# Merged row-half groups and two-block runs of the heads' products in a gated mix of linear attention and a SwiGLU FFN

## The chip, the cores and the metric

One core of a Trainium2 (trn2) chip runs one program. The metric is its time on the device in microseconds, the median of several executions. Five engines work beside each other, each through its own queue in order: TensorE (PE, with its weight loads PEld), VectorE (DVE), ScalarE (ACT), GpSimd (POOL), and SyncE (SP), which here only issues DMAs. They wait for one another by semaphores. PE writes to PSUM, eight banks of 128 partitions by 512 f32 values; POOL can't read it, so ACT and DVE empty it.

## The reference

For 2048 tokens of 640 features (bf16), two branches are mixed by a gate:

```
q, k, v = split(x @ wqkv)                      # 32 heads of 20
phi(q)  = [softmax(q w_phi), softmax(-q w_phi)]   # 40 features per head; the same for k
kv = sum over tokens of phi(k)^T v ;  z = sum over tokens of phi(k)
o  = (phi(q) kv) / (phi(q) z + 1e-6)
a  = o @ wo
b  = (silu(x @ w_gate) * (x @ w_up)) @ w_down     # 1728 hidden values
g  = sigmoid(sum(x * gate_w))
out = g * a + (1 - g) * b
```

## The kernel before

**Order by hand.** The kernel is written out step by step. `ORDER` is a list of letters with indices; each letter calls one function, which records its instructions on the engines, and a tracker adds the semaphore waits that the addresses call for. So the list sets the order in each engine's queue, and nothing reorders it later. All matmuls are recorded by `mm` (L300), all ACT operations by `actop` (L318), DVE and POOL operations by `copy` (L324), `tt` (L328), `stt` (L332) and `reduce` (L339), all DMAs by `dma` (L353, L354).

**Tiles and blocks.** Tokens go in 16 tiles of 128; four tiles make a block, counted from 0 to 3. The first part (until the letter Z) loads, makes the values (V) and the keys' features (K, S, P), and sums kv and z (E). The part from Z on, which the change touches, has these steps:

- Q t: the queries' products of tile t on PE (ten matmuls of 320 columns) and two exponentials on ACT into eq. A, B, C: sums and products on DVE (`qsum`, `qden`, `qscale`; C is six DVE instructions, ending in qc). c: the scaling on POOL into ph, and a transposing DMA on SP into phiT, which has room for two blocks.
- F b.k: chunk k (128 of the 1728 hidden values) of the FFN for block b: ten matmuls of 512 columns into a pair of banks, tanh and a copy on ACT, a product on DVE and one on POOL, into hT (128 x 512). hT has two buffers of 14 chunks, for blocks of even and odd number. Chunk 13 has only 64 hidden values; its tokens are laid in both row halves of the chunk (two tiles in rows 0 to 63, two in rows 64 to 127).
- O b.p and o b: the heads' products phi(q) kv of block b, part p of three. Each head pair fills only 64 columns of the array, so two matmuls run side by side on the column halves. The result goes to oT by ACT. The odd last group (40 columns) goes to ol, and o issues four small DMAs on SP that move it into oT.
- W b.p: chunk 13's down projection for two tiles of a block. Its contraction is 64 rows long, so two matmuls, one for each tile, run side by side on the row halves. W opens the accumulation of the two tiles: it takes a pair of PSUM banks for each, which D keeps adding to.
- D b.u: down projection of tile u of block b: 13 chunks against wd and 5 groups of oT against wog, each in two parts of 320 columns, then ACT's scaling by the gate into osb and the store on SP. Tile 15 ends the kernel; its second part is cut into 224 and 96 columns, to shorten the last eviction.

PSUM's eight banks are used as four pairs; a step takes the pair used longest ago (`next_pair`). In before, W stands eight times (two per block), and the O's of a block stand together, so there are four runs of them. A stage of F's is followed by a stage of D's of a block, block after block.

Of the kernel before, what the change touches and what calls it, by code (L numbers as in the profile page):

```python
# [1 line left out]

# [1 line left out]

# [4 lines left out]
P = 128  # L9
S_TOK = 2048  # L10
D = 640
# [4 lines left out]
NB = 4  # L16
# [25 lines left out]
U0.3 U1.3 U2.3 U0.4 U1.4 U2.4 V3 Y F0.1 M1 i3 M0 F0.0 M2 V4 M3 M4 K0 K1 I S0 V6 V5 S1 P0 K3 K2 P1 E0  # L42
V9 K4 E1 S3 V7 P3 K5 S2 V8 V10 S4 P2 P4 E2 R0 E3 K6 S5 P5 S6 i4 E4 V14 K7 K8 P6 V15 S7 R2 E5 K9 S8
P7 R1 E6 K10 S9 V12 P8 E7 P9 K11 S10 P10 F0.2 R3 F1.2 E8 E9 K12 E10 S11 S12 K14 S14 V11 K13 P11 P12
E11 K15 P14 R4 S13 P13 F1.9 S15 P15 E12 V13 T F1.8 E13 F1.11 E14 Q1 E15 Q0 Q2 N Z A1 A0 J A2 F0.7
F0.9 F1.4 B0 F1.12 B1 F0.4 L C0 F1.7 c0 F1.10 C1 F0.5 B2 c1 F0.11 Q3 C2 F1.0 F0.8 c2 F0.10 B3 Q4
F1.6 A3 C3 Q5 c3 F1.3 F0.13 F0.12 A4 F0.3 B4 F1.5 F0.6 O0.2 O0.1 O0.0 o0 C4 F1.1 F1.13 B5 A5 C5 Q6
c4 Q7 c5 Q8 W0.0 B7 A6 B6 C6 A7 c6 D0.1 D0.0 Q9 C7 W0.1 B8 A8 D0.2 C8 c7 Q10 D0.3 F2.10 F2.9 F2.2 c8
O1.2 A9 O1.1 B9 O1.0 B10 F2.8 o1 C9 Q11 c9 F2.5 F2.11 F2.4 Q12 B11 F2.3 A10 C10 B12 F2.7 A11 C11
W1.1 D1.3 D1.2 A12 c11 c10 Q14 W1.0 D1.0 A14 C12 D1.1 Q13 F3.2 F3.3 c12 O2.2 O2.1 B13 B14 O2.0 o2  # L50
F2.13 A13 F3.12 F3.5 F2.1 C14 Q15 F3.4 F3.9 F2.12 C13 F2.0 A15 c13 F2.6 c14 B15 F3.1 F3.0 F3.6 C15
c15 F3.13 W2.0 F3.7 D2.1 D2.0 F3.11 O3.2 O3.0 O3.1 F3.8 o3 F3.10 W2.1 D2.3 W3.0 D3.0 D3.1 D2.2 W3.1
D3.2 D3.3
"""


# [143 lines left out]
def _build(nc, A_x, A_wqkv, A_w_phi, A_wo, B_x, B_w_gate, B_w_up, B_w_down, gate_w, out):  # L200
# [5 lines left out]
    def sb(name, shape, dtype):  # L206
        t = nc.alloc_sbuf_tensor(name, list(shape), dtype)
        tr.reg(t, "sbuf", nc.lookup_mloc(t).addr)
        return t
# [9 lines left out]
    ident = sb("ident", [P, P], BF16)  # L219
    us = sb("us", [P, 3, 512], BF16)  # L220
    osb = sb("osb", [P, 4, D], BF16)
    ol = sb("ol", [P, 256], BF16)
    kvsb = sb("kvsb", [P, NCH, 64], BF16)
    hmask = sb("hmask", [P, 3], F32)
    zt = sb("zt", [P, NCH, 3], F32)
# [16 lines left out]
    qd = sb("qd", [P, 2, 32], F32)  # L242
    qc = sb("qc", [P, 2, 66], F32)
    hT = sb("hT", [P, 2, 14, 512], BF16)

    wdbase = nc.lookup_mloc(wd).addr
    v1x = nc.alloc_sbuf_tensor_at("v1x", [P, NT - NV, 33 * 21], BF16, offset=wdbase)
    tr.reg(v1x, "sbuf", wdbase)

    def vbuf(t):  # L250
        return v1r[:, t, :] if t < NV else v1x[:, t - NV, :]
# [28 lines left out]
    def bank(b, c0, c1, r0=0, r1=P):  # L280
        return ps[r0:r1, b * 512 + c0:b * 512 + c1]
# [62 lines left out]
    def memset(e, a, v):  # L344
        eo = tr.eng[e]
        return run(e, lambda: eo.memset(a, v), [], [a])
# [67 lines left out]
    def fills(i):  # L414
        if i < 2:
            v1v = (v1r, v1x)[i][:, :, :].rearrange("p b (h d) -> p b h d", d=DH + 1)
            memset("pool", v1v[:, :, H, :], 0.0)
            memset("pool", v1v[:, :, :, DH:DH + 1], 1.0)
        elif i == 2:
            memset("pool", ekr[:, :, 1280:FK], 0.0)  # L420
            memset("pool", krec[:, :, :], 0.0)
        elif i == 3:
            memset("pool", kvsb[:, :, :], 0.0)
            memset("pool", eq[:, :, 1280:FP], 0.0)
            memset("pool", qc[:, :, :], 0.0)
            memset("pool", hmask[:, :], 1.0)
            select(hmask[:, :], [[-40, 3]], ALU.is_ge, 0.0, 0, 1)
            select(hmask[:, :], [[40, 3]], ALU.is_gt, 0.0, 40, -1)
        else:
            memset("pool", ph[:, :, :], 0.0)  # L430
            memset("pool", zh[:, NCH:P], 0.0)
# [225 lines left out]
           ALU.mult)  # L657
        dma("sp", phiT[:, (t // 4) % 2, t % 4, :, :], ph[:, b, :], transpose=True)

    def oitem(bt, part):  # L660
        buf = bt % 2
        pr = next_pair()
        pairs = []
        ms = [2 * part, 2 * part + 1]
        for i, m in enumerate(ms):
            for s in range(2):
                j = 2 * m + s
                if j >= NCH:
                    continue
                if j == NCH - 1:  # L670
                    for g, p0 in enumerate((0, 64)):
                        pairs.append((bank(2 * pr + i, 256 * g, 256 * g + 256, p0, p0 + 40),
                                      kvsb[0:80, j, 0:40], phiT[0:80, buf, 2 * g:2 * g + 2, j, :],
                                      True, True, False))
                    continue
                else:
                    l, o = kvsb[0:120, j, :], bank(2 * pr + i, 0, 512, 64 * s, 64 * s + 64)
                    r = phiT[0:120, buf, :, j, :]
                pairs.append((o, l, r, True, True, False))
        mm(pairs)  # L680
        if part < 2:
            copy("act", oT[:, buf, 2 * part:2 * part + 2, :], halves(pr, 512))
        else:
            copy("act", oT[:, buf, 4, :], bank(2 * pr, 0, 512))
            copy("act", ol[0:40, :], bank(2 * pr + 1, 0, 256, 0, 40))
            copy("act", ol[64:104, :], bank(2 * pr + 1, 256, 512, 64, 104))

    def omove(bt):
        for g in range(2):
            for s in range(2):  # L690
                dma("sp", oT[64 * s + 60:64 * s + 64, bt % 2, :, 256 * g:256 * g + 256],
                    ol[64 * g + 20 * s:64 * g + 20 * s + 20, :])


    nus = [0]

    def fitem(bt, k):
        buf = bt % 2
        pr = next_pair()
        xr = [xT[:, 4 * bt:4 * bt + 4, c, :] for c in range(5)]  # L700
        u = us[:, nus[0] % 3, :]
        nus[0] += 1
        if k < 13:
            g, up = bank(2 * pr, 0, 512), bank(2 * pr + 1, 0, 512)
            h = hT[:, buf, k, :]
            mm(group(g, [(wg[:, c, P * k:P * k + P], xr[c]) for c in range(5)]))
            mm(group(up, [(wu[:, c, P * k:P * k + P], xr[c]) for c in range(5)]))
        else:
            pairs = []
            for b in range(2):  # L710
                pairs += group(bank(2 * pr + b, 0, 256),
                               [(wt[:, c, P * b:P * b + P], xT[:, 4 * bt + b:4 * bt + 4:2, c, :]) for c in range(5)])
            mm(pairs)
            for b in range(2):
                r0, r1 = 64 * b, 64 - 64 * b
                h, g = hT[r0:r0 + 64, buf, k, 0:256], bank(2 * pr + b, 0, 256, r0, r0 + 64)
                actop(h, g, ACTF.Tanh, 0.5)
                actop(u[r0:r0 + 64, 0:256], bank(2 * pr + b, 0, 256, r1, r1 + 64), ACTF.Copy)
                stt(h, h, 1.0, g, ALU.add, ALU.mult)
            h = hT[:, buf, k, 0:256]  # L720
            tt("pool", h, h, u[:, 0:256], ALU.mult)
            return
        if bt == 2:
            for _ in range(NWAIT):
                act.wait_ge(tr.sem["pe"], 1)
        actop(h, g, ACTF.Tanh, 0.5)
        actop(u, up, ACTF.Copy)
        stt(h, h, 1.0, g, ALU.add, ALU.mult)
        tt("pool", h, h, u, ALU.mult)
# [8 lines left out]

    def parts(t):

        pr = dpr[t]
        if t < NT - 1:
            return [(2 * pr[0], 0, 320), (2 * pr[0] + 1, 320, D)]
        return [(2 * pr[0], 0, 320), (2 * pr[0] + 1, 320, 544), (2 * pr[1], 544, D)]

    def hitem(bt, p):

        todo = []
        for b in range(2):
            t = 4 * bt + 2 * p + b  # L750
            dpr[t] = [next_pair() for _ in range(1 + (t == NT - 1))]
            held.update(dpr[t])
            r = slice(64 * b, 64 * b + 64)
            todo.append([(bank(k, 0, c1 - c0), hT[r, bt % 2, 13, P * p:P * p + P], wd[r, 13, c0:c1], True, False, False)
                         for k, c0, c1 in parts(t)])
        mm([m for ab in zip_longest(*todo) for m in ab if m])

    def ditem(bt, u):
        buf = bt % 2
        t = 4 * bt + u  # L760
        tok = slice(P * u, P * u + P)
        ls = [(hT[:, buf, k, tok], wd[:, k, :]) for k in range(13)]
        ls += [(oT[:, buf, m, tok], wog[:, m, :]) for m in range(5)]
        n = len(ls)
        cols = [[(bank(k, 0, c1 - c0), l, r[:, c0:c1], False, i == n - 1, False) for i, (l, r) in enumerate(ls)]
                for k, c0, c1 in parts(t)]
        held.difference_update(used(r) for r in dpr[t])
        o = osb[:, t % 4, :]
        if t < NT - 1:
            mm([p for ab in zip(*cols) for p in ab])  # L770
            actop(o.rearrange("p (b c) -> p b c", b=2), halves(dpr[t][0]), ACTF.Copy, omg[:, t:t + 1])
            stores_done()
            out_evs.append(dma("sp", out2[t * P:(t + 1) * P, :], o))
            return
        for (b, c0, c1), e, ms in zip(parts(t), ("sp", "sp", "act"), cols):
            mm(ms)
            if e == "act":
                run("dve", lambda: dve.tensor_scalar(o[:, c0:c1], bank(b, 0, c1 - c0), omg[:, t:t + 1], None,  # L778
# [11 lines left out]
    def kv_end():  # L790
# [9 lines left out]
        "f": lambda i: load_ffn(FCUT[i], FCUT[i + 1]), "L": load_late_weights, "T": tail_weights, "J": gates,  # L800
        "Y": w_blocks, "I": kv_begin, "N": kv_end, "Z": z_row,
        "Q": qtile, "A": qsum, "B": qden, "C": qscale, "c": qmul,
        "F": fitem, "O": oitem, "o": omove, "W": hitem, "D": ditem,
    }
    for w in LOADS.split() + ORDER.split():
        ops[w[0]](*[int(a) for a in w[1:].split(".") if a])
# [45 lines left out]
```

## Time and profile before

| what | us |
|---|---|
| median of 3 runs | 287.82 |
| lowest and highest | 287.75 and 288.12 |
| the profiled execution | 289.13 |
| its span, from the first instruction to the last | 287.8 |

The page gives each engine's busy time with its share of the span, and the chain that ended last, followed back from the last instruction to whatever released each step. A row of a group or of the timeline reads: line, engine, operation, output<-inputs, shape, count; in the timeline start and length stand in front. A shape such as 64*128 is the part of the array that a matmul uses: rows by columns. Matmuls overlap each other in the pipeline, so the length of one (379 ns for 512 columns) is more than the distance to the next start, which is what it costs. The granted clock is 1.00 throughout.

### The profile page before, as it was taken

The page shows a single profiled execution, that of the slowest core. Times are in us where ns is not written, and L with a number is a line of the kernel's source. Part 1 is how long each engine was busy: PE and PEld are TensorE (multiplying, and loading weights), DVE is VectorE, ACT ScalarE, POOL GpSimd, SP SyncE. Part 2 cuts the span into 40 slices and gives each one's busy share as a digit, 9 for nine tenths or more (in the row PEclk, how much of TensorE's full clock was granted, in tenths as well). Part 3 has the DMA queues.
Part 4 walks back from the last instruction along what each step waited for, and adds up shares of the span by engine and source line. Part 5 has one row for each costly group of instructions (what it writes and reads, how often), then busy time and mean ns, then how long its engine had stood idle before and what let it go on. Part 6 is the DMA issues. An engine that isn't in the chain of part 4 may idle for free.

```text
span 287.8 us, 5041 instructions
## 1 busy us (share of the span) xinstructions
PE 283.5 (98%) x1999; PEld 173.5 (60%) x1999; DVE 169.8 (59%) x247; ACT 152.9 (53%) x264; POOL 156.9 (55%) x125
## 2 busy tenths in 40 slices
PE   7899999999999999999999999999999999999997
PEld 6567777675644555456675445767544457556766
DVE  2145757577479998769992787952566983010000
ACT  0668768766665557684434865132786543541112
POOL 8154899979635778947170757260465696130000
DMA  7985789000037264202243022051020053000101
GB/s 232 160 115 120 118 220 363 9 0 3 0 109 248 69 133 76 50 4 50 57 120 73 2 56 52 25 110 38 23 53 4 3 101 73 25 4 26 46 23 48
DMA packets 49374, 21.87 MB, mean 76 GB/s; under 512 B 39462, under 2 KB 49214, under 8 KB 49350
## 3 DMA queue, kind: packets, MB, share of 16 engines
q1 hardware_dynamic: 47830, 20.67, 31.5%
q10 hardware_dynamic: 1520, 0.87, 1.0%
q8 instruction: 16, 0.26, 0.4%
q14 instruction: 8, 0.07, 0.1%
HBM read 9.38 MB, written 2.62 MB: 42 GB/s over the span
## 4 chain that ended last, share of the span: by engine, by line
PE 96%; DMA 2%; ACTq 0%; DVE 0%; issue 0%
PE ps L300 96%; DMA xs<-in_A_x_dram 2%; ACTq L354 0%; PE ps L312 0%; DVE osb L778 0%
## 5 line engine op out<-in xcount | busy, mean ns | idle before, releaser
L328 POOL TENSOR_TENSOR hT<-hT,us 128x512 bf16<-128x512 bf16 (+1 forms) x56 | 66.2, 1193 | 68.4 <-ACT us L318 35.2
L332 DVE SCALAR_TENSOR_TENSOR hT<-hT,ps 128x512 bf16<-128x512 bf16 (+1 forms) x60 | 38.2, 648 | 50.8 <-ACT hT L318 45.0
L300 PE MATMUL ps<-xT,wg 128*128 128x512 bf16 x260 | 64.6, 379 | 0.0
L300 PE MATMUL ps<-xT,wu 128*128 128x512 bf16 x260 | 64.6, 379 | 0.0
L300 PE MATMUL ps<-wd,hT 128*128 128x320 bf16 (+3 forms) x462 | 62.6, 295 | 0.0
L300 PEld LDWEIGHTS ps<-wd,hT 128*128 128x128 bf16 (+1 forms) x462 | 41.8, 98 | 19.2 <-issue 3.1
L328 POOL TENSOR_TENSOR ph<-eq,qc 128x1320 bf16<-128x1320 bf16 x16 | 40.4, 2530 | 15.8 <-DVE qc L645 15.8
L300 PE MATMUL ps<-wqk,xT 128*128 128x320 bf16 x320 | 47.7, 299 | 0.0
L318 ACT ACTIVATE hT<-ps 128x512 bf16<-128x512 f32 (+1 forms) x60 | 34.0, 567 | 20.4 <-PE ps L300 15.2
L300 PEld LDWEIGHTS ps<-xT,wu 128*128 128x128 bf16 x260 | 25.5, 98 | 30.7
L318 ACT ACTIVATE us<-ps 128x512 bf16<-128x512 f32 (+1 forms) x60 | 34.1, 569 | 18.1 <-PE ps L300 17.2
L328 POOL TENSOR_TENSOR ekr<-ekr,krec 128x1280 bf16<-128x1280 bf16 x16 | 37.4, 2360 | 8.2 <-DVE krec L342 8.2
L300 PEld LDWEIGHTS ps<-xT,wg 128*128 128x128 bf16 x260 | 24.9, 98 | 27.7 <-ACT oT L318 1.2
L318 ACT ACTIVATE osb<-ps,omg 128x640 bf16<-128x640 f32 (+2 forms) x17 | 12.9, 758 | 53.0 <-PE ps L300 53.0
L300 PEld LDWEIGHTS ps<-wqk,xT 128*128 128x128 bf16 x320 | 30.6, 98 | 12.4
L318 ACT ACTIVATE eq<-ps 128x640 bf16<-128x640 f32 x32 | 22.5, 704 | 18.5 <-POOL ph L328 8.5
L339 DVE TENSOR_REDUCE ksum<-ekr 128x64 f32<-128x1280 bf16 x16 | 23.5, 1470 | 11.6 <-ACT ekr L318 11.6
L318 ACT ACTIVATE ekr<-ps 128x640 bf16<-128x640 f32 x32 | 22.3, 704 | 8.6 <-PE ps L300 8.1
L339 DVE TENSOR_REDUCE qz<-eq 128x64 f32<-128x1280 bf16 x16 | 23.6, 1478 | 3.6 <-ACT eq L318 3.6
L300 PE MATMUL ps<-wvg,xT 128*128 128x320 bf16 (+1 forms) x160 | 24.1, 300 | 1.2 <-DMA wvg<-in_A_wqkv_dram 1.1
L300 PE MATMUL ps<-wog,oT 128*128 128x320 bf16 (+2 forms) x165 | 24.7, 295 | 0.0
L339 DVE TENSOR_REDUCE qw<-ez 128x64 f32<-128x1280 bf16 x16 | 23.6, 1478 | 0.0
(73 smaller groups left out, 196.6 us busy)
## 6 DMA issues: line engine op xcount, KB each, us to landing
out_dram<-osb SPq DMA_DIRECT2D x15, 160.0 KB, 1.8
wd<-in_B_w_down_dram SPq DMA_DIRECT2D x1, 2080.0 KB, 10.4
wg<-in_B_w_gate_dram SPq DMA_DIRECT2D x1, 1040.0 KB, 10.0
wu<-in_B_w_up_dram SPq DMA_DIRECT2D x1, 1040.0 KB, 12.1
wg<-in_B_w_gate_dram SPq DMA_DIRECT2D x1, 800.0 KB, 6.1
wu<-in_B_w_up_dram SPq DMA_DIRECT2D x1, 800.0 KB, 7.6
wog<-in_A_wo_dram SPq DMA_DIRECT2D x2, 375.0 KB, 4.2
xs<-in_A_x_dram ACTq DMA_DIRECT2D x3, 160.0 KB, 3.9
```

The lines of the kernel that those rows point to most:

```text
L300: last = pe.matmul(o, lhsT=l, rhs=r, start=st, stop=sp_, skip_group_check=sk)
L318: return run("act", lambda: act.activation(o, i, func, scale=scale), rd, [o])
L328: return run(e, lambda: eo.tensor_tensor(o, a, b, op), [a, b], [o])
L332: return run("dve", lambda: dve.scalar_tensor_tensor(out=o, in0=a, scalar=s, in1=b, op0=op0, op1=op1), rd, [o])
L339: return run("dve", lambda: dve.tensor_reduce(o, i, AX.X, ALU.add), [i], [o])
```

## The change

W now stands once per block. It closes the accumulation of the block's tiles 0 and 1 (which D has opened) and opens that of tiles 2 and 3 (which D closes), in one group of eight matmuls. The O's become `orun`: for two blocks at once, part by part, with the second bank of each item copied by DVE instead of ACT, then the moves of both blocks; ol gets a buffer per block. For two blocks to be ready, the FFN values of block 2 and of the first six chunks of block 3 get memory of their own: hx, laid over the values' buffer (v1r), the value weights (wvg) and the key half of wqk, which are not read any more by then. ORDER is new from Z on: O of blocks 0 and 1 as one run, then their D's, O of blocks 2 and 3, then theirs. In a D, the 26 matmuls with wd and the ten with wog are recorded as two groups, so that the wait for oT stands at the second. Tile 15's third part takes chunk 13 as a full matmul from hz, a zeroed buffer whose lower half gets that tile's 64 rows.

```diff
-... Q2 N Z A1 A0 J A2 F0.7
-F0.9 F1.4 B0 F1.12 B1 F0.4 L C0 F1.7 c0 ...
-F1.6 A3 C3 Q5 c3 F1.3 F0.13 F0.12 A4 F0.3 B4 F1.5 F0.6 O0.2 O0.1 O0.0 o0 C4 F1.1 F1.13 B5 A5 C5 Q6
-c4 Q7 c5 Q8 W0.0 B7 A6 B6 C6 A7 c6 D0.1 D0.0 Q9 C7 W0.1 B8 A8 D0.2 C8 c7 Q10 D0.3 F2.10 ...
-c15 F3.13 W2.0 F3.7 D2.1 D2.0 F3.11 O3.2 O3.0 O3.1 F3.8 o3 F3.10 W2.1 D2.3 W3.0 D3.0 D3.1 D2.2 W3.1
-D3.2 D3.3
+... Q2 N A1 A0 Z F2.8 F2.10 J
+A2 F0.8 B0 F1.10 C0 c0 F0.7 F0.5 F2.2 B2 F0.9 C2 F1.3 L Q3 F1.4 A3 F3.3 F1.13 c2 B1 F1.12 C1 B3 Q5
...
+A6 Q7 C5 c5 F3.0 F2.1 C6 c6 F1.0 F0.10 Q8 B7 A7 F1.5 F0.4 C7 c7 B8 Q9 F0.11 F2.11 A8 F2.12 A9 B9
+F0.12 Q10 F2.4 F3.4 O0.2 F3.5 C8 A10 c8 F0.13 D0.0 Q11 D0.1 B10 W0 D0.3 C9 A11 C10 c9 c10 B11 Q12
+Q13 B12 C11 c11 D0.2 A12 C12 c12 D1.1 Q14 A13 A14 B13 C13 c13 Q15 B14 B15 D1.0 W1 A15 C14 c14 D1.3
+C15 c15 D1.2 F3.6 F2.13 F3.7 F3.10 F3.9 F3.12 F3.8 O2.4 F3.11 F3.13 D2.1 D2.0 W2 D2.3 D2.2 D3.0 D3.1
+W3 D3.2 D3.3
@@ buffers
-    ol = sb("ol", [P, 256], BF16)
+    ol = sb("ol", [P, 2, 256], BF16)
+    hz = sb("hz", [P, P], BF16)
+    for i, (a, rel, n) in enumerate(((v1r, 0, 8), (wvg, 0, 6), (wqk, 5 * D * 2, 6))):
+        base = nc.lookup_mloc(a).addr + rel
+        hx.append(nc.alloc_sbuf_tensor_at("hx%d" % i, [P, n, 512], BF16, offset=base))
+    def hbuf(bt, k):
+        if bt == 2:
+            return hx[k // 8][:, k % 8, :]
+        if bt == 3 and k < 6:
+            return hx[2][:, k, :]
+        return hT[:, bt % 2, k, :]
@@ fills
+            memset("pool", hz[:, :], 0.0)
@@ oitem, orun
+        e = "dve" if two else "act"
+        copy("act", oT[:, buf, 2 * part, :], bank(2 * pr, 0, 512))
         if part < 2:
-            copy("act", oT[:, buf, 2 * part:2 * part + 2, :], halves(pr, 512))
+            copy(e, oT[:, buf, 2 * part + 1, :], bank(2 * pr + 1, 0, 512))
         else:
-            copy("act", oT[:, buf, 4, :], bank(2 * pr, 0, 512))
-            copy("act", ol[0:40, :], bank(2 * pr + 1, 0, 256, 0, 40))
-            copy("act", ol[64:104, :], bank(2 * pr + 1, 256, 512, 64, 104))
+            copy(e, ol[0:40, buf, :], bank(2 * pr + 1, 0, 256, 0, 40))
+            copy(e, ol[64:104, buf, :], bank(2 * pr + 1, 256, 512, 64, 104))
+    def orun(b0, b1):
+        for part in range(3):
+            for b in range(b0, b1):
+                oitem(b, part, b1 - b0 > 1)
+        for b in range(b0, b1):
+            omove(b)
@@ hitem, ditem
+        for p in range(2):
+            todo = []
+            for b in range(2):
+                t = 4 * bt + 2 * p + b
+                if p:
+                    d_open(t)
+                r = slice(64 * b, 64 * b + 64)
+                todo.append([(bank(k, 0, c1 - c0), hbuf(bt, 13)[r, P * p:P * p + P], wd[r, 13, c0:c1], p == 1, p == 0, False)
+                             for k, c0, c1 in parts(t)])
+            mm([m for ab in zip(*todo) for m in ab])
+        for t in (4 * bt, 4 * bt + 1):
+            held.remove(used(dpr[t]))
+            d_out(t)
+        if bt == NB - 1:
+            copy("dve", hz[64:P, :], hbuf(bt, 13)[64:P, P:2 * P])
...
-            mm([p for ab in zip(*cols) for p in ab])
+            both = [p for ab in zip(*cols) for p in ab]
+            mm(both[:26])
+            mm(both[26:])
...
+        ps3 = parts(t) + [(2 * next_pair(), 544, D)]
+        cols.append(group(bank(ps3[2][0], 0, D - 544), [(l, r[:, 544:D]) for l, r in [(hz[:, :], wd[:, 13, :])] + ls]))
```

## What was predicted

> **What bounds the kernel now.** I read the page first, then the chain of waits, then the timeline of TensorE (PE) around one run of each kind that the change merges. The page's first lines and its chain:
>
> ```profile
> span 287.8 us, 5041 instructions
> ## 1 busy us (share of the span) xinstructions
> PE 283.5 (98%) x1999; PEld 173.5 (60%) x1999; DVE 169.8 (59%) x247; ACT 152.9 (53%) x264; POOL 156.9 (55%) x125
> ...
> PE 96%; DMA 2%; ACTq 0%; DVE 0%; issue 0%
> ```
>
> To be seen: PE is busy 98% of the span and is itself 96% of the chain that ends last, while the others are near 60%. From 10 us on PE has no idle row. So the time is a sum of matmul slots, the distance from one start to the next: in the trace 216 ns for 512 columns, 136 for 320, 109 for 256. Only two things move the time: fewer or cheaper slots, or a wait in a chain that has none. The timeline, PE alone, around W2.0 (FFN chunk 13, on row halves):
>
> ```profile
> 233.50 1.26 PE L300 MATMUL ps<-xT,wt 128*128 128x256 bf16 x10
> 234.68 0.45 PE L300 MATMUL ps<-wd,hT 64*128 64x320 bf16 x4
> 235.06 1.25 PE L300 MATMUL ps<-xT,wg 128*128 128x512 bf16 x5
> ```
>
> Ten slots of 109 end at 234.59, and W starts at 234.68: **0.09 us lost going in**. Its four matmuls run as two side-by-side pairs, 2 x 0.136 = 0.27, and would end at 234.95; the next starts at 235.06: **0.11 lost going out** (by single starts: 142 to 144 ns between the pairs where a plain slot is 136, then 228, that is 92 over a slot). The matmul after that comes 10 ns late (226 for 216). In all 0.095 + 0.092 + 0.010, about 0.20 us per W beside the 7 ns inside. The seven other W groups show the same to 4 ns. Now the first run of the heads' products (O, on column halves):
>
> ```profile
> 121.69 1.24 PE L300 MATMUL ps<-xT,wu 128*128 128x512 bf16 x5
> 122.86 1.38 PE L300 MATMUL ps<-phiT,kvsb 120*64 120x512 bf16 x12
> 124.18 1.25 PE L300 MATMUL ps<-xT,wg 128*128 128x512 bf16 x5
> 125.27 1.24 PE L300 MATMUL ps<-xT,wu 128*128 128x512 bf16 x5
> ```
>
> From 121.69 five slots of 216 end at 122.77, O starts at 122.86: 0.09. Inside are five pairs of 512 and one of 256: 5 x 0.216 + 0.109 = 1.19 of the 1.32 until 124.18; of the 0.13 over, 0.02 lies beside the narrow pair and stays with it. With the 10 ns of the next matmul, a run costs **0.20 us** beyond its slots. All four runs agree.
>
> **The change, part by part.**
>
> *Row-half groups, eight to four.* The slots stay: W of a block now has four pairs where two W's had two each. Four groups less, 4 x 0.20 = **-0.80**. Inside a merged W I take 138 ns per pair; the rows bound it by 136 and 143, and all twelve inner steps differ by 0.08 us at most. Tile 15's third part (96 columns) leaves the row halves, where it stood alone, and becomes one full matmul with the zero-padded copy hz: 43 ns out, 43 in. The copy to hz (64x128; the 128x128 COPY row is 221 ns) is on VectorE (DVE), which has nothing else to do during the last D's, and is used three D's later. The memset of hz (205 ns, by the row of ident's) stands on POOL before chunk F0.0's product, followed by P0, which waits for krec: 8.2 us of POOL's idle time ends there. Without that cover it would be 0.2 us, once, early.
>
> *Heads' products, four runs to two.* Same matmuls, same two odd pairs per two blocks, two runs less: 2 x 0.20 = **-0.40**.
>
> *Evictions inside a run.* Six items now follow each other, 0.43 us each (the last two 0.33), and PSUM has four pairs of banks: item 4 writes where item 0 was, item 5 where item 1 was. ScalarE (ACT) takes the first bank of each, DVE the second. ACT: six 128x512 copies, 0.48 apart, 0.59 long (rows). A DVE copy of 512 from f32 PSUM has no row. These stand nearest, in the groups by shape:
>
> ```profile
> L324 DVE CAST wqk<-ps 128x640 bf16<-128x640 f32 x2 | 1.6, 824 | 2.2 <-PE ps L300 2.2
> L328 DVE TENSOR_TENSOR kvsb<-ps,hmask 120x160 bf16<-120x160 f32 x3 | 0.8, 309 | 0.0
> L324 DVE COPY xT<-ps 128x512 bf16<-128x512 bf16 x3 | 1.3, 425 | 0.0
> ```
>
> Below, 0.43 us (same width, bf16); above, 0.82 (same kind, wider). From 160 to 640 columns is 515 ns, so 512 columns take 0.69, the value I take, being nearest the CAST; 0.60 from start to start, as the 684 ns FFN product on DVE starts every 598 when it is back to back. The clock from the run's first matmul: item 0 is done at 0.43 + 0.20, DVE's copies end at 1.32 and 1.92. Item 4 is due at 1.73 and item 5 at 2.05, after 0.05 for the semaphore: slack 0.36 and **0.08**. So no wait, but barely. At 0.82 long and as far apart, item 5 waits 0.27: **0 to +0.54** for two runs. At the low end nothing is gained, since PE then waits for nothing either way.
>
> The Trainium skill, "TensorEngine Tiling (Array Packing)", PSUM Bottleneck, speaks against a longer run: tiling makes TensorE faster but not the emptying of PSUM. The copies above are this case's answer: shared between ACT and DVE they cost 0 to 0.54. Left to ACT alone (1.02 us per pair by the oT row, six in 2.4 us), the rule would have decided.
>
> *Moves of the odd head.* ol now has a buffer per block, and eight small moves, not four, stand in SP's queue at once. In before's trace a second move into the same columns issues 2.15 us after the first (126.71, 128.86). D0.0 needs the first two only (token columns 0 to 255). DVE finishes block 0's ol copies 1.5 us after the run's end (4 x 0.60, then two at 0.2 to 0.42); the second move issues 2.15 later and, as that wait tells, takes about 2.0 to land: 5.7 after the run. D0.0's products with oT are due after F3.5 (2.16), F0.13 (1.09) and D0.0's own 26 matmuls (3.53), 6.9 with the way out: **slack 1.2, cost 0**. The run of blocks 2 and 3 has F3.11 and F3.13 ahead of D2.1, the same slack. Behind the eight moves stand the transpose of tile 8 and three stores; tile 8's phiT is read only in the second run, some 50 us later.
>
> *FFN values of blocks 2 and 3 (counted from 0) in dead buffers, and the new order.* No instruction more; it lets 38 FFN chunks stand between Z and the first O. Does an engine fall behind? From Z to that O, row by row: PE 92 us; DVE 37 products x 0.60, eight A (1.48), ten B (1.37), eight C (3.23) = 74; POOL 37 x 1.22 + eight products of 2.53 = 66; ACT 57. In the last eight chunks before O PE takes 20.0 and DVE 13.7. From O to F3.6 (eight D, five Q) it is PE 53, DVE 47, POOL 22. The tightest, DVE, has 6 us to spare in each: 0.
>
> *Sum.* -0.80 - 0.40 = -1.20. The profiled execution's span is 287.84 (its own time 289.13, 1.3 around it), so the span becomes 286.6; the runs' median, 287.82, is as long as that span, and becomes **286.6 us**, 0.4% less.
>
> One more weighing: the skill's "TensorE: Matmul & The Clock Gate", Part 2, step 4, gives a drain of some 128 cycles; at its 2.4 GHz that is an estimate of 53 ns per switch. Twelve switches less would then be worth 0.64, not 1.20. The trace shows 92 to 95 at every switch, and the row decides.
>
> **Rivals.**
>
> *DVE's copies hold the run* (same side, less gain): slack 0.08 is all that speaks against it; at the bound 286.6 + 0.54 = 287.2. Together with a DVE that comes late by half a chunk (0.3) to each run it is 287.3 to 287.7, no change.
>
> *The merge does not save the switch*: were each half of a merged W to pay a switch of its own, where accumulation ends on tiles 0 and 1 and opens on 2 and 3, only O's 0.40 would stay: 287.4. Against it, the second pair inside every W of before, in other banks, comes after 143 ns, not 230.
>
> *Slower, by the moves*: if the two moves land 2.1 us later than reckoned, each run leaves PE waiting 2.1 - 1.2 = 0.9, twice 1.8, which eats 1.2 and 0.58 more: 288.4. From a delay of 1.2 it costs, from 1.8 the gain is gone. For it: in two of the four runs of before the gap between such moves was 2.5 to 2.6. Against: that is 0.5, not 2.1, and no transpose or store stands ahead of them that isn't long gone.
>
> **How the numbers follow.** About 0.2%, 0.58 us, is what a measurement of this kernel tells from no change: faster ends at 287.24, slower begins at 288.40. The forecast, 286.3 to 286.9: 0.72. DVE holds the run: 0.15 (0.11 below 287.24, 0.04 above). The merge fails: 0.04, no change. The moves: 0.05 (0.04 slower, 0.01 no change). Other waits in the new order: 0.04, faster still. So faster 0.87, same 0.09, slower 0.04. The range goes from 286.3 (the sum less 0.3; the runs shown lie 0.37 apart) to 287.3, the bound of the copies.
>
> **What would show it.** Right: PE without idle rows after 10 us; in the timeline four groups of eight 64*128 matmuls and two runs of 24 heads' matmuls, each with 0.09 ahead and 0.1 behind. Wrong: a gap inside a run before its fifth or sixth item, released by DVE's oT copy (the copies are dearer); a gap inside a D between its wd and its wog matmuls, released by the DMA oT<-ol (the moves); 228 ns in the middle of a W (the merge); PE waiting for DVE or POOL ahead of the first O (the order).

## The result, and the profile after

| what | before | after |
|---|---|---|
| median, us | 287.91 (6 runs) | 286.53 (6 runs) |
| lowest and highest, us | 287.5 and 288.29 | 286.28 and 286.76 |
| profiled execution, us | 289.13 | 286.63 |
| its span, us | 287.8 | 285.4 |

Ratio 0.9953, with a 95% interval from 0.9942 to 0.9964: faster by 1.4 us (1.0 to 1.7), where the forecast was 286.6 and 1.2.

First the page of the kernel after: span, busy time by engine, and the chain by engine.

```profile
span 285.4 us, 5063 instructions
PE 282.6 (99%) x1999; PEld 175.1 (61%) x1999; DVE 176.0 (62%) x264; ACT 146.9 (51%) x256; POOL 157.3 (55%) x126
...
PE 99%; DVE 0%; issue 0%
```

PE's matmuls are as many as before (1999), and they are again nearly the whole chain. DVE is busy 6 us longer and ACT 6 us shorter, mostly the heads' copies. None of that is on the chain.

The two spans differ by 2.5 us, twice the forecast. The chain of waits tells how that splits (start, length, what). First before, its last pieces, which were not shown yet:

```profile
9.59 69.27 PE ps L300 x640
...
78.91 207.01 PE ps L300 x1294
```

And after:

```profile
8.49 69.18 PE ps L311 x640
...
77.72 205.74 PE ps L311 x1294
```

Read the lengths, not the starts. The last piece, 1294 matmuls from Z to the end, is the part that the change touches: 207.01 to 205.74, that is 1.27 shorter, against a forecast of 1.20. The 640 matmuls ahead of it, which the change doesn't touch, are alike to 0.1. The other 1.1 us lie in front: they start at 9.59 in the one execution and at 8.49 in the other. That is not the change's doing: the start was at 8.1 to 8.7 in all eight experiments (8.10 in e5, which is built on the kernel before), and the executions of before that ran beside the experiments have a span of 286.6 in the median, 1.2 shorter than the profiled one. Below, **the stretch** is that last piece, 1294 matmuls without an idle row unless one is shown; to the nanosecond it is 207.007 before and 205.733 after.

The timeline of PE in the kernel after, around the first two-block run:

```profile
168.30 1.24 PE L311 MATMUL ps<-xT,wu 128*128 128x512 bf16 x5
169.47 2.57 PE L311 MATMUL ps<-phiT,kvsb 120*64 120x512 bf16 x24
171.98 1.25 PE L311 MATMUL ps<-xT,wg 128*128 128x512 bf16 x5
...
175.24 3.69 PE L311 MATMUL ps<-wd,hT 128*128 128x320 bf16 x26
178.77 1.52 PE L311 MATMUL ps<-wog,oT 128*128 128x320 bf16 x10
```

The run has 24 matmuls where it had 12, and there are two of them. From its start to the next group it takes 171.98 - 169.47 = 2.51. Its slots are 10 x 0.216 + 2 x 0.109 = 2.38, so 0.13 is over: exactly what a run of half that length had over. Ahead of it 0.09 is lost again (five slots of 216 from 168.30 end at 169.38). No row has an idle time: neither DVE's copies nor the moves, which the products with wog at 178.77 wait for, stop PE. The merged row-half group of the last block, also in the kernel after:

```profile
271.71 1.11 PE L311 MATMUL ps<-wog,oT 128*128 128x320 bf16 x7
272.76 0.71 PE L311 MATMUL ps<-wd,hT 64*128 64x320 bf16 x8
273.40 1.80 PE L311 MATMUL ps<-wd,hx 128*128 128x320 bf16 x12
```

Seven slots of 136 from 271.71 end at 272.66, and four pairs from 272.76 would end at 273.30: 0.10 is lost on either side, once for eight matmuls. There are four such groups. DVE and ACT around the first two-block run of the kernel after (in brackets the idle time before, and what ended it); first DVE:

```profile
169.13 0.69 DVE L343 SCALAR_TENSOR_TENSOR hx<-hx,ps 128x512 bf16<-128x512 bf16 x1 [1.22 <-ACT hx L329]
170.14 2.48 DVE L335 CAST oT<-ps 128x512 bf16<-128x512 f32 x4 [0.32 <-PE ps L311]
172.54 1.78 DVE L335 CAST ol<-ps 40x256 bf16<-40x256 f32 x4
```

then ACT:

```profile
170.14 3.04 ACT L329 ACTIVATE oT<-ps 128x512 bf16<-128x512 f32 x6
```

DVE comes to the run with 0.32 us of idle time before it, so it is not behind. Its four copies of 512 take 2.48, and the run's last item starts before they are over. How close that is comes under the experiments.

### The profile page after: what moved, and what is told of

Same layout as the page of the kernel before. It is cut to its first block, busy times and chain, and to the rows that moved or that the text cites. A ratio compares the mean times of both kernels' runs of the same rounds, so it can differ in the third digit from the quotient of the medians.

```text
span 285.4 us, 5063 instructions
## 1 busy us (share of the span) xinstructions
PE 282.6 (99%) x1999; PEld 175.1 (61%) x1999; DVE 176.0 (62%) x264; ACT 146.9 (51%) x256; POOL 157.3 (55%) x126
## 4 chain that ended last, share of the span: by engine, by line
PE 99%; DVE 0%; issue 0%
PE ps L311 97%; PE ps L497 1%; PE ps L323 1%; DVE osb L822 0%
## 5 line engine op out<-in xcount | busy, mean ns | idle before, releaser
L339 POOL TENSOR_TENSOR hT<-hT,us 128x512 bf16<-128x512 bf16 (+1 forms) x36 | 43.8, 1224 | 24.3 <-DVE hT L343 15.1
L311 PE MATMUL ps<-wd,hT 128*128 128x320 bf16 (+3 forms) x295 | 40.2, 296 | 0.0
L343 DVE SCALAR_TENSOR_TENSOR hT<-hT,ps 128x512 bf16<-128x512 bf16 (+1 forms) x39 | 24.8, 642 | 20.0 <-ACT hT L329 14.4
L311 PEld LDWEIGHTS ps<-wd,hT 128*128 128x128 bf16 (+1 forms) x295 | 26.9, 98 | 11.1 <-issue 1.3
L339 POOL TENSOR_TENSOR hx<-hx,us 128x512 bf16<-128x512 bf16 (+1 forms) x20 | 23.0, 1159 | 14.2 <-ACT us L329 8.9
L329 ACT ACTIVATE hT<-ps 128x512 bf16<-128x512 f32 (+1 forms) x39 | 21.9, 563 | 15.6 <-PE ps L311 11.0
```

The source lines that it names most:

```text
L311: last = pe.matmul(o, lhsT=l, rhs=r, start=st, stop=sp_, skip_group_check=sk)
L329: return run("act", lambda: act.activation(o, i, func, scale=scale), rd, [o])
L339: return run(e, lambda: eo.tensor_tensor(o, a, b, op), [a, b], [o])
L343: return run("dve", lambda: dve.scalar_tensor_tensor(out=o, in0=a, scalar=s, in1=b, op0=op0, op1=op1), rd, [o])
```

## The experiments

The theory: PE is never let wait, so the stretch is the sum of its slots and of a price for each switch of the array between whole and halves; with one switch in and one out that is about 0.20 us per group. The rivals: the gain came from the new order and buffers; DVE's copies or the moves have more room than reckoned, or none; matmuls on halves are cheap by themselves, and the switch is not what they cost. All the ratios are to the kernel before, run beside it. The stretch is compared, being free of the start's spread.

**a0: the kernel after, once more.** No edit.

> The changed kernel itself once more, beside the others: 286.5 us against 287.9; PE's stretch from the transpose of z to its last matmul 205.74 again. If the 1.1 us by which the first profile's start was shorter than that of the kernel before belongs to single executions and not to the change, the start until the first stretch without idle rows now differs from 8.49 us by some tenths while the rest stays.

Stretch 205.735, the same as in the first profile of this kernel to 2 ns. Median 286.67 (286.1 to 287.28, 11 runs), ratio 0.9947 (0.9926 to 0.9968). The stretch is a far finer measure than the time: 2 ns against a range of 1.2 us between executions. The 640 matmuls ahead of it start at 8.44, where the first profile had 8.49; the tenths of difference that were expected here did not show.

**e1: the row-half groups of blocks 0 to 2 in two again.** Seven groups instead of four; buffers and runs as after.

```diff
-... B10 W0 D0.3 ... D0.2 A12 ...
+... B10 W0.0 D0.3 ... D0.2 W0.1 A12 ...
@@ the same for W1 and W2; hitem, ditem
-        for p in range(2):
+        for p in (range(2) if h == 2 else (h,)):
...
-        if u < 2:
+        first = u < 2 or bt < NB - 1
+        if first:
             d_open(t)
```

> The changed kernel, with the row-half group of blocks 0, 1 and 2 cut in two again (tiles 0 and 1 closed after their D's, tiles 2 and 3 after theirs), so seven groups instead of four; all else as in the change. Switch theory (each separate group on a part of the array costs 95 ns going in, 92 + 10 going out, and the first inner pair 7 more): PE's stretch from the transpose of z to its last matmul grows by 3 x 0.20 = 0.6 us (205.74 to 206.35), the time from 286.53 to 287.1. Rival, that the gain of the change came from the new order or from buffers that no longer hold anyone up: 0, since order and buffers stay. Rival, that a group pays by its matmuls and not by being one: 0, since there are as many.

Stretch 206.368, 0.635 longer: 0.212 for each of the three groups. Median 287.52, ratio 0.9976 (0.9961 to 0.999). In the timeline of this kernel the second group of block 1 (W1.1) is to be seen:

```profile
221.71 1.39 PE L311 MATMUL ps<-wog,oT 128*128 128x320 bf16 x9
223.03 0.45 PE L311 MATMUL ps<-wd,hT 64*128 64x320 bf16 x4
223.40 0.82 PE L311 MATMUL ps<-xT,wg 128*128 128x512 bf16 x3
```

Nine slots of 136 from 221.71 end at 222.93: 0.10 lost on the way in. Two pairs would end at 223.30, and the next matmul starts at 223.40: 0.10 on the way out. In the kernel after, the same wog group goes over to the same wg group without a loss:

```profile
221.71 1.11 PE L311 MATMUL ps<-wog,oT 128*128 128x320 bf16 x7
222.66 1.24 PE L311 MATMUL ps<-xT,wg 128*128 128x512 bf16 x5
```

Seven slots of 136 from 221.71 end at 222.66. The order and the buffers of the change were all in e1, and the gain of these groups was gone: it is the switches'.

**e2: each block's heads' products as a run of its own**, DVE's copies kept.

```diff
-... O0.2 F3.5 C8 ...   ... O2.4 F3.11 F3.13 ...
+... O0 F3.5 O1 C8 ...  ... O2 F3.11 O3 F3.13 ...
-    def orun(b0, b1):
+    def orun(b):
         for part in range(3):
-            for b in range(b0, b1):
-                oitem(b, part, b1 - b0 > 1)
-        for b in range(b0, b1):
-            omove(b)
+            oitem(b, part, True)
+        omove(b)
```

> The changed kernel, with each run of the heads' products cut in two by one FFN chunk (O of block 0, F3.5, O of block 1; O of block 2, F3.11, O of block 3), copies still shared by ACT and DVE: four runs instead of two. Switch theory: two runs more at 0.20, plus 0.02 each if the extra 21 ns belong to the first pair of any run and not to the narrow pair as the prediction had it: PE's stretch grows by 0.40 to 0.44 us (205.74 to 206.14-206.18), the time to 286.9-287.0. Rival (order and buffers): 0. In the trace 237 ns after the first pair of each of the four runs says that the 21 ns belong to the run.

Stretch 206.183, 0.450 longer: 0.225 for each of two runs. Median 286.94, ratio 0.9973 (0.9951 to 0.9995). Its timeline of PE:

```profile
168.46 1.24 PE L311 MATMUL ps<-xT,wu 128*128 128x512 bf16 x5
169.63 1.38 PE L311 MATMUL ps<-phiT,kvsb 120*64 120x512 bf16 x12
170.94 1.25 PE L311 MATMUL ps<-xT,wg 128*128 128x512 bf16 x5
...
173.20 1.38 PE L311 MATMUL ps<-phiT,kvsb 120*64 120x512 bf16 x12
174.52 1.27 PE L311 MATMUL ps<-xT,wt 128*128 128x256 bf16 x10
```

A run of 12 takes 1.31 and 1.32 from start to next group, against slots of 1.19: 0.13 over, as the run of 24 has. By single starts, always from the first matmul of a pair to the first of the next (its second starts 3 to 4 ns after the first), the 0.13 is 24 ns at the first pair (240 instead of 216) and 101 on the way out. The first pair takes 240 ns in every run of the kernels before, after and e2, and the narrow pair 113 to 114, where a slot of its width is 109. So nearly all of the 0.02 belongs to the run, and one run more costs 0.225, not 0.20.

**e3: all the copies of a run left to ACT**, as in before.

```diff
-                oitem(b, part, b1 - b0 > 1)
+                oitem(b, part, False)
```

> The changed kernel, with all copies of the heads' products on ACT (two banks in one copy of 1.02 us, 0.91 apart), so that DVE no longer shares them. Theory that the long run only goes through because two engines empty PSUM: item 5 is due 2.05 us after the run's start and finds its banks free at 2.56 + 0.05, waiting 0.56; the chunk after it waits about 0.5 more for item 2's banks: 1.0 per run, 2.1 us in all (time 288.6, slower than before the change). Rival, that four pairs of banks are enough whoever empties them: 0 (286.5).

Stretch 207.870, 2.137 longer, and slower than before: median 288.74, ratio 1.0033 (1.0021 to 1.0046). The timeline of PE:

```profile
169.17 2.26 PE L311 MATMUL ps<-phiT,kvsb 120*64 120x512 bf16 x20
171.82 0.52 PE L311 MATMUL ps<-phiT,kvsb 120*64 120x512 bf16 x4 [0.40 <-ACT oT L329]
172.74 1.25 PE L311 MATMUL ps<-xT,wg 128*128 128x512 bf16 x5 [0.40 <-ACT oT L329]
```

Twenty matmuls go through, for PSUM's four pairs take that many while ACT empties the first. The sixth item waits for ACT (0.56 late by single starts, as expected), and so does the FFN chunk behind the run, each after 0.40 without a matmul. About 1.07 per run is lost. The merge of the runs is worth 0.45, and with ACT alone on the copies the long runs lose 2.14, nearly five times that.

**e4: one DVE copy of each run made twice**, the one that the fifth item waits for.

```diff
-            copy(e, oT[:, buf, 2 * part + 1, :], ...)
+            for _ in range(2 if part == 0 and buf == 0 else 1):
+                copy(e, oT[:, buf, 2 * part + 1, :], ...)
```

> The changed kernel, with DVE's copy of item 0 of each two-block run made twice (same values), so that every later DVE copy of the run comes 0.60 us later. If the slack of the run's fifth and sixth item is 0.36 and 0.08 us, they wait 0.24 and 0.28 or a little more: 0.5 to 0.65 us per run, 1.0 to 1.3 us in all (287.5 to 287.8). Rival, that ACT or something else sets when the banks come free and DVE has more room than reckoned: under 0.3 us in all.

Stretch 207.089, 1.356 longer, 0.678 for each run; median 288.16, ratio 1.0005 (0.9993 to 1.0016), that is the whole gain. The timeline of PE:

```profile
169.16 1.92 PE L311 MATMUL ps<-phiT,kvsb 120*64 120x512 bf16 x16
171.29 1.11 PE L311 MATMUL ps<-phiT,kvsb 120*64 120x512 bf16 x8 [0.22 <-DVE oT L335]
```

The wait is ahead of the fifth item, released by DVE's copy, and there is one more ahead of the sixth. The loss is a little over the 1.0 to 1.3 that was expected. Two things account for it. The repeated copy started 0.726 after the first one, not 0.60: it started when the first had ended, where the later ones start 0.08 before that (that it is so because it writes the same buffer was not tried). And PE starts again dearly: the weight load stands at 171.294 and its matmul at 171.295, the matmul takes 403 ns instead of 379, and from this pair's first matmul to the next pair's it is 240, not 216. That is the same 24 ns as at the start of every run. By single starts the fifth item waited 0.386 and the sixth 0.244; with 24 ns after each that is the 0.678. The fifth waited 0.386 after DVE had lost 0.726, so it had had a slack of 0.34; the sixth, by the same count, 0.07.

**e5: in the kernel before, the row-half groups of blocks 0 and 1 merged alone.** Six groups instead of eight, heads' products in four runs on ACT, no new buffers. Q9, Q14 and the D's of block 1 stand elsewhere, so that banks are free for the merged groups, and a D's matmuls are recorded as two groups, as in the change.

```diff
-Q8 W0.0 B7 ... D0.1 D0.0 Q9 C7 W0.1 B8 A8 D0.2 C8 ...
+Q8 B7 ... D0.1 D0.0 W0.2 C7 B8 A8 D0.2 Q9 C8 ...
-W1.1 D1.3 D1.2 A12 ... Q14 W1.0 D1.0 A14 C12 D1.1 Q13
+D1.1 A12 c11 c10 D1.0 W1.2 D1.3 Q14 A14 C12 D1.2 Q13
```

> The kernel before, with the row-half groups of blocks 0 and 1 alone merged (six groups instead of eight; Q9 and Q14 moved by one D so that a free pair of banks is there); no buffer of the change, no merged run of the heads' products, no other order. Switch theory: 2 x 0.20 = 0.40 us less: PE's stretch from the transpose of z to its last matmul 206.6 instead of 207.01, the time 287.5 against 287.9. Rival (the gain needs the new order or the buffers): 0, 287.9.

The stretch by the chain of waits of this kernel:

```profile
77.34 206.58 PE ps L300 x1294
```

That is 207.01 to 206.58, 0.43 shorter, 0.215 for each group. Median 287.48 against 287.91, ratio 0.9986 (0.9962 to 1.0009): the time alone doesn't tell it from no change, the stretch does. A merge gives the same in before's order as in the new one.

**e6: no row halves at all.** Chunk 13 as full matmuls against two copies of its weights, each zero in the other half of the rows; W's go.

```diff
-... O0.2 F3.5 C8 A10 c8 F0.13 D0.0 ... B10 W0 D0.3 ...
+... O0.2 F0.13 F3.5 C8 A10 c8 D0.0 ... B10 D0.3 ...
@@ ditem, for every tile
+        ls += [(hbuf(bt, 13)[:, P * (u // 2):P * (u // 2) + P], wd2[:, :] if u % 2 else wd[:, 13, :])]
```

> The changed kernel without any row-half group: chunk 13 goes as a full matmul for each tile, against two copies of its weights, each with zeros in the other row half; F0.13 stands ahead of F3.5. Each block has eight slots of 136 (1.09 us) instead of a group with four slots and its switches (0.75). Switch theory: 4 x 0.34, less the hz matmul's 0.04: 1.3 us more than the changed kernel (PE's stretch 207.0, the time 287.8), about what the kernel before took with eight groups. Rival, that the switches were not the cost and pairing saves what it seems to, four slots of 136 per block: 4 x 0.54 = 2.2 us more (288.7).

Stretch 207.122, 1.389 longer, of which 0.10 is a wait of F0.13 behind the first run. The rest, 1.29, is what the sum of slots says: per block eight full slots for four pairs and a group's switches, 8 x 0.136 - 4 x 0.136 - 0.212 = 0.33, four times, less the 0.04 of the hz matmul, which isn't needed here. Median 287.9, ratio 0.9992 (0.997 to 1.0013). Read against the kernel before, this prices the old form: a group of two pairs saves 2 x 0.136 = 0.27 and pays 0.21 for it. By this sum eight such groups were worth 0.5 us in all.

**e8: the first move of blocks 0 and 2 made twice**, so that the one that D waits for comes 2 us later.

```diff
-            for s in (0, 1):
+            for s in ((0, 0, 1) if g == 0 and bt % 2 == 0 else (0, 1)):
```

> The changed kernel, with the first move of ol into oT of blocks 0 and 2 issued twice (same bytes), so that the second move, for which the first D of each run of blocks waits, lands 2.15 us later. If the slack is 1.2 us, PE waits 0.9 ahead of the wog matmuls of D0.0 and of D2.1, 1.8 us in all (288.3). Rival, that the moves have more room than reckoned (over 2.2 us): 0 (286.5).

Stretch 207.447, 1.714 longer; median 288.25, ratio 1.0005 (0.9984 to 1.0025). The timeline of PE:

```profile
175.14 3.69 PE L311 MATMUL ps<-wd,hT 128*128 128x320 bf16 x26
179.58 1.53 PE L311 MATMUL ps<-wog,oT 128*128 128x320 bf16 x10 [0.74 <-DMA oT<-ol]
```

And its chain of waits, which now goes through the moves:

```profile
173.34 2.15 DMA oT<-ol
175.49 0.02 issue
175.50 2.02 DMA oT<-ol
177.53 0.02 issue
177.54 1.99 DMA oT<-ol
179.54 0.05 issue
179.58 58.68 PE ps L311 x402
```

Each move into the same columns waits for the one before it, 2.0 to 2.15 us. D0.0's 26 matmuls from 175.14 end their slots at 178.68. The second move, the last that D0.0 waits for in the kernel after, had landed at 177.53: a slack of 1.1. The third lands at 179.53, and PE starts at 179.58, 0.9 late; the second run's D loses 0.78. (The bracket shows 0.74, as it counts from the modelled end of the last matmul, not from its slot's.)

## Why the prediction was right

It was right in the mechanism and within 0.1 us in the time; both terms of its sum were a little too small. By its steps:

- **The bound.** PE's slots set the end before and after. All the delays that were put in came out of the sum to some 0.1 us, and waits appeared only where they had been put in, but for the 0.10 in e6.
- **Row-half groups, -0.80.** A group measured 0.212 (e1) and 0.215 (e5), so the term was mis-sized by 0.012 each. The prediction counted from the second matmul of a pair, which starts 3 to 4 ns after the first, and left out the 7 ns "inside" a W. From first matmul to first matmul a group in the trace of before loses 95 ns going in, 11 at its first pair (147 instead of 136), 96 going out and 10 at the matmul after: 0.212. All four terms go with the group. A second step was wrong too: "43 ns out, 43 in". In before the 96-column matmul of the last group lay mostly beside the 320 columns in the other row half: by single starts that group of five took 380 ns to the next matmul, the groups of four 378. So 2 ns went out and 43 came in. The traces of before and after give -0.81 for all the groups; that this is so near to -0.80 is in part luck, as the two errors, 0.05 and 0.04, cancel. The loss that the rival foresaw in the middle of a merged group isn't there: its pairs take 147, 136 and 136 ns, and only the last, 228 to 232, leads out.
- **Heads' runs, -0.40.** One run more measured 0.225 (e2), so two are 0.45. The step that failed is "0.02 lies beside the narrow pair and stays with it". It goes with the run, as the 240 ns of each run's first pair show. The rest is rounding: the prediction's own 0.09, 0.13 less 0.02, and 0.01 make 0.21. In the traces the four runs of before lose 0.231 to 0.234 each and the two of after 0.234, so the change took 0.46. With the -0.81 of the groups that is the 1.27 measured.
- **The copies, 0 with 0.08 to spare.** The row that had been missing, from the groups by shape of the kernel after:

```profile
L335 DVE CAST oT<-ps 128x512 bf16<-128x512 f32 x8 | 5.0, 682 | 0.6 <-PE ps L311 0.6
L335 DVE CAST ol<-ps 40x256 bf16<-40x256 f32 x8 | 3.4, 419 | 0.2
```

  682 ns, against the 0.69 that was interpolated between a TENSOR_TENSOR and a CAST row, and 0.60 from start to start. The COPY row of the same width, 425, with its bf16 source, would have been far off. The sixth item starts at 171.553 and the copy that it waits for ends at 171.427; less the 0.05 of the semaphore 0.08 is left, as reckoned (0.07 by e4). The fifth had 0.34 (e4), reckoned 0.36. The narrow copies were put between 0.2 and 0.42 and take the upper end, 0.42.
- **The moves, slack 1.2.** e8 shows 1.1, and the price beyond it: 0.9 for a move of 2.0. The rival "slower, by the moves" had the right size and the wrong premise: one more move is the delay that it needed, and none came.
- **The new order, 0.** No idle row of PE ahead of the first run, and DVE reaches it with idle time.
- **The span, 286.6.** This was missed by 1.2, as the profile shown of before was an execution whose 640 matmuls began 1.1 later than in the profile of after, and 0.9 to 1.5 later than in the experiments. The median was forecast from the difference, and so was not touched.

Two rules of the Trainium skill were weighed. "TensorEngine Tiling (Array Packing)", PSUM Bottleneck, says that tiling speeds up TensorE but not the emptying of PSUM, and to use both engines for that: e3 shows the rule decide, at +2.14 us with ACT alone, and the kernel after shows that two engines suffice, with 0.08 to spare. The drain of some 128 cycles in "TensorE: Matmul & The Clock Gate", Part 2, step 4, which the page gives for the end of a matmul and not for a switch, came to an estimate of 53 ns per switch. The traces of before, after and e2 show 92 to 101 at each switch, and the experiments 106 to 113 with what the first pair and the matmul behind a group add. By the estimate the sum would have been 0.64, half of the 1.27 measured.

## What to carry to other kernels

When PE bounds a kernel without idle time, each separate group on halves of the array costs a fixed price (here 0.21 to 0.225 us), so count the slots that it saves against it, and merge groups until PSUM's emptying or a buffer stops it. A longer run fills PSUM faster than one engine empties it: reckon, item by item, when each bank is free again, and give the copies to two engines. Compare the stretch that the change touches, not the spans of two single executions, whose first microseconds differ by more than such a change.

## What the runs showed of the hardware

- **The first slot after a switch or a wait is longer.** Counted from first matmul to first matmul, the first pair of 512 columns on column halves takes 240 ns instead of 216, after each switch and after the waits in e3 and e4. The first pair of 320 columns on row halves takes 145 to 147 instead of 136, and so does the first full matmul of that width behind a group and after the waits of e8 (147).
- **The first weight load after a switch isn't ahead of its matmul.** Among full matmuls a weight load starts together with the matmul before, 134 to 136 ns ahead of its own for 320 columns. At every switch in the traces of before, after and e2, and after the waits of e4 and e8, it stands only 0 to 5 ns ahead. Whether the longer first slot, or the 92 to 101 ns of a switch, come from that was not tried.
- **Pairs on column halves keep the pace of full matmuls:** 215 to 216 ns for 512 columns inside a run, from one pair's first matmul to the next pair's (218 to 219 for the one behind the narrow pair).
- **The start moves, the rest doesn't.** The 640 matmuls ahead of Z begin between 8.1 and 9.6 us in the ten profiles, and take 69.2 to 69.3 from there, but for e8, which has an idle 0.15 in it; the stretch of the kernel after, profiled twice, repeats to 2 ns. What delays the first DMAs was not studied.
